# Attention values and low parts of weights on GpSimd, and another order of the opening, in a linear attention and two-MoE kernel

## The chip, the cores and the metric

The kernel runs on one core of one Trainium2 chip. The metric is the device time of one execution in microseconds, from the median of several runs. Everything is in fp32; the large matmuls work on operands split into a high and a low part (fp32r), three products for each.

## What is computed

A gated linear attention (4 batches, 8 heads, 768 positions, 48 channels), then a mixture of 4 experts, then a second feed-forward layer. Setup and shapes are left out:

```python
    for t in range(S):
        state = alpha[:, :, t, :, None] * state + np.einsum('bhd,bhe->bhde', k[:, :, t], v[:, :, t])
        y[:, :, t] = np.einsum('bhd,bhde->bhe', q[:, :, t], state)
...
    x = attn_out.transpose(0, 2, 1, 3).reshape(3072, 384)
    p = domain_probs / (domain_probs.sum(-1, keepdims=True) + 1e-09)
    for e in range(4):
        out += p[:, e:e + 1] * (np.maximum(x @ w1[e], 0.0) @ w2[e])
...
    h = out @ w_in
    return (h * np.clip(h + 3.0, 0.0, 6.0) / 6.0) @ w_out
```

## The kernel before

The attention is cut into 12 units of 256 positions of one batch (`n` = 0 to 11). The state recurrence of a unit is unrolled as a tree: chunks of 8 positions in each partition are worked out elementwise (`chunk`), and the levels above (4, 8, 16, 32 chunks of positions, `tree`) by small matmuls on TensorE, with masks and scalings between them.

The pieces have short names, and strings of names fix their order. In `chunk`: `p0` to `p3` are products of q and k of the innermost three levels, `r0` to `r2` their sums over channels (a reduction, `dg`), `u0`, `u1`, `kk`, `kq`, `tp` scale q and k by alpha for the next level, `cp` copies on ACT, and `y0` to `y5` multiply the values `v` by those sums and add them into `y8`. In `tree`: `T_tp`, `T_k0`, `T_k1`, `T_q0`, `T_q1` transpose on TensorE and copy out of PSUM (ACT; for `qt` of unit 0 VectorE, line 326), `tls` makes products of the gates, `Sc` copies one level's operands (ACT), `C` are that level's matmuls, `Su` scales `kt` and `qt` (VectorE, line 356), `M` multiplies the mask in, `K` transposes the scaled keys, `U` makes the state updates, `Y` brings `y8` into PSUM, `L` adds the levels, `Z` carries the state on, `ST` adds the state's share, `X` orders the copies behind it, `A` stores the unit's result into `x_d` in DRAM, `R` loads it back as MoE input, and `XS` splits it into high (ACT, line 775) and low part (VectorE, line 776).

The MoE goes in three phases over slices of 256 hidden columns. Phase 0 handles the first seven slices of weights (`S0`) while the attention runs: in each step one `mm1` (9 matmuls into `ph`), the relu on ACT into `hh` (line 808), `hl` on VectorE (line 811), and `mm2` of the step before (9 matmuls into `po`). Between the steps stands one group of attention pieces (`GROUP`, `BETWEEN`) and its `rest` (`CHUNK`), seven groups to a unit. The first two periods of 14 steps have 256 token columns each and the later ones 512; two units belong to a period. In the first period the weights also arrive: `load_w`, then `split_w`, whose high part is copied on ACT (line 756) and whose low part VectorE subtracts (line 757), one of 14 such tiles a step from the second step on. They are loaded into the two buffers of `rawp` and four pieces of room lent by x's tiles (`early`, `again`).

Inside the manual schedule (line 916) VectorE, ACT, TensorE and SP carry out their instructions in program order; GpSimd's few (masks, memsets, later two multiplications of `decode`) are ordered by the scheduler. All DMAs are issued by SP, which waits in order too. The opening (lines 949 to 983) is written out by hand: unit 0 from beginning to end, then the elementwise part of unit 1, with `busy(n)` for n idle matmuls (each of two passes) that keep TensorE going. `raw` tiles of q, k, alpha and v have one buffer each, so that the next unit's load waits for the last reader.

Of the kernel before, what the change touches and what calls it, by code (L numbers as in the profile page):

```python
# [18 lines left out]
P = 128  # L19


class Attention:
# [29 lines left out]
        "-X tls", "Sc0 Su0", "Sc1 Su1", "Sc2 M0 Su2", "Sc3 Su3", "M2", "Z0 Z1 Z2 Z3",  # L52
    )
    CHUNK = (
        "y0 y1 y2 y3 y4 y5", "-A +p0 +r0", "+p1 +p2 +r1", "-R +u0", "+u1 +cp +kk +kq", "+tp +p3 +r2", "-XS",
    )

    def __init__(self, ctx, tc, q, k, v, alpha, y_d, psum_pool, psum_tag, reload, split):
# [97 lines left out]
    def chunk(self, n):  # L156

        nc, D = self.nc, self.D  # L160
        ve = nc.vector
        tt = ve.tensor_tensor
        r = self.rawt[n]
        wtags = ("w", "w", "w") if n else ("asb0", "w", "asb1")
        mul, add = ALU.mult, ALU.add
        y8 = self.y8.rearrange("p i h d -> p h i d")[:, :, :, 0:D]
        st = {}

        def hm(ap, w):
            return ap.rearrange("p h (m w) d -> p (h m) w d", w=w)  # L170

        q, k, a = r["q"], r["k"], r["a"]
        q2, k2, a2 = hm(q, 2), hm(k, 2), hm(a, 2)
        q4, k4 = hm(q, 4), hm(k, 4)

        def wtile(x):
            cols = 1024 if wtags[x].startswith("asb") else 768
            w = self.wk.tile([P, cols], F32, tag=wtags[x], name=f"w{x}_{n}")[:, 0:768]
            st[x] = w
            return w  # L180

        def ptile(x):
            return self.wk.tile([P, 768], F32, tag="pr", name=f"pr{x}_{n}")

        def padded(t, h, part):

            return t.rearrange("p (m w) h d -> p h m w d", w=4)[:, h, :, 2 * part : 2 * part + 2, 0:D]

        def p0():
            tt(wtile(0).rearrange("p (h i d) -> p h i d", h=2, d=D), q, k, op=mul)  # L190

        def p1():
            tt(q, q, a, op=mul)

        def p2():

            tt(wtile(1)[:, 0 : 8 * D].rearrange("p (x d) -> p x d", d=D), q2[:, :, 1, :], k2[:, :, 0, :], op=mul)

        def u0():
            tt(q2[:, :, 1, :], q2[:, :, 1, :], a2[:, :, 0, :], op=mul)  # L200

        def u1():
            tt(k2[:, :, 0, :], k2[:, :, 0, :], a2[:, :, 1, :], op=mul)
            st["t1"] = self.wk.tile([P, 8, D], F32, tag="t1", name=f"t1_{n}")
            tt(st["t1"], a2[:, :, 0, :], a2[:, :, 1, :], op=mul)

        def cp():
            for h in range(2):
                nc.scalar.copy(padded(self.kp, h, 1), k4[:, 2 * h : 2 * h + 2, 2:4, :])
                nc.scalar.copy(padded(self.qp, h, 0), q4[:, 2 * h : 2 * h + 2, 0:2, :])  # L210

        def side(z, zp, y):
            t1v = st["t1"].rearrange("p (x w) d -> p x w d", w=2)
            for h in range(2):
                hs = slice(2 * h, 2 * h + 2)
                tt(
                    padded(zp, h, 1 - y),
                    z[:, hs, 2 * (1 - y) : 2 * (1 - y) + 2, :],
                    t1v[:, hs, y, :].unsqueeze(2).to_broadcast([P, 2, 2, D]),
                    op=mul,  # L220
                )

        def kk():
            side(k4, self.kp, 1)

        def kq():
            side(q4, self.qp, 0)

        def tp():
            tpv = self.tp.rearrange("p x h d -> p h x d")[:, :, :, 0:D]  # L230
            t1h = st["t1"].rearrange("p (h x w) d -> p h x w d", h=2, w=2)
            tt(tpv, t1h[:, :, :, 0, :], t1h[:, :, :, 1, :], op=mul)

        def p3():

            wv = wtile(2).rearrange("p (x t s d) -> p x t s d", x=4, t=2, s=2)
            for i in range(2):
                tt(
                    wv[:, :, i],
                    q4[:, :, 2 + i, :].unsqueeze(2).to_broadcast([P, 4, 2, D]),  # L240
                    k4[:, :, 0:2, :],
                    op=mul,
                )

        def reduced(x, n_):
            dg = self.wk.tile([P, 16], F32, tag=f"dg{x}", bufs=2, name=f"dg{x}_{n}")
            ve.tensor_reduce(
                dg[:, 0:n_], st[x][:, 0 : n_ * D].rearrange("p (x d) -> p x d", d=D), op=add, axis=AX.X
            )
            st[f"dg{x}"] = dg  # L250

        def y0():
            tt(y8, r["v"], st["dg0"].rearrange("p (h i) -> p h i", h=2).unsqueeze(3).to_broadcast([P, 2, 8, D]), op=mul)

        def y1():
            pv = ptile(0)[:, 0 : 8 * D].rearrange("p (x d) -> p x d", d=D)
            tt(pv, hm(r["v"], 2)[:, :, 0, :], st["dg1"][:, 0:8].unsqueeze(2).to_broadcast([P, 8, D]), op=mul)
            yv = y8.rearrange("p h (m w) d -> p h m w d", w=2)[:, :, :, 1, :]
            tt(yv, yv, pv.rearrange("p (h m) d -> p h m d", h=2), op=add)

        def y2():
            st["pv"] = ptile(1).rearrange("p (x t s d) -> p x t s d", x=4, t=2, s=2)
            y3_(0)

        def y3_(i):
            dv = st["dg2"].rearrange("p (x t s) -> p x t s", t=2, s=2)
            tt(st["pv"][:, :, i], hm(r["v"], 4)[:, :, 0:2, :], dv[:, :, i, :].unsqueeze(3).to_broadcast([P, 4, 2, D]), op=mul)

        def y3():
            y3_(1)  # L270

        def y4():
            pv = st["pv"]
            tt(pv[:, :, :, 0, :], pv[:, :, :, 0, :], pv[:, :, :, 1, :], op=add)

        def y5():
            yv = y8.rearrange("p h (m w) d -> p h m w d", w=4)
            pw = st["pv"].rearrange("p (h m) t s d -> p h m t s d", h=2)
            for i in range(2):
                tt(yv[:, :, :, 2 + i, :], yv[:, :, :, 2 + i, :], pw[:, :, :, i, 0, :], op=add)  # L280

        return dict(
            p0=p0, p1=p1, p2=p2, p3=p3, r0=lambda: reduced(0, 16), r1=lambda: reduced(1, 8),
            r2=lambda: reduced(2, 16), u0=u0, u1=u1, cp=cp, kk=kk, kq=kq, tp=tp,
            y0=y0, y1=y1, y2=y2, y3=y3, y4=y4, y5=y5,
        )

# [3 lines left out]
    def tree(self, n):  # L291
# [196 lines left out]
        def A():  # L488
            for j in range(2):
                ys = wk(f"ys{j}", [P, NP, P])  # L490
                nc.scalar.copy(ys, s["py"][j])
                for h in range(2):
                    nc.sync.dma_start(
                        self.y_d.rearrange("(r h e) t -> h e r t", r=NP, h=2)[h][:, :, n * U + P * j : n * U + P * j + P],
                        ys[64 * h : 64 * h + D],
                    )
# [32 lines left out]
    def rest(self, g):  # L529
        n, k = divmod(g, self.H)  # L530
        self.run(n, self.CHUNK[k])

        if k == 1:
            self.load(n + 1, "v")
            self.load_vt(n)
        if k == 5:
            self.load(n + 2, "qka")
            self.load_vd(n + 1)
# [3 lines left out]
def tile_gla__then__moe__then__moe2(  # L542
# [206 lines left out]
    def split_w(y, i, eng):  # L749
        raw = raws.pop((y, i))  # L750
        pool = wpb if S0 <= i < S0 + SB or S1 <= i < S1 + SB else wpa
        hi, lo = (pool.tile([P, 3 * SL], F32R, tag=f"w{y}{z}", name=f"w{y}{z}_{i}") for z in "hl")
        if eng is nc.gpsimd:
            eng.tensor_copy(hi, raw)
        else:
            nc.scalar.copy(hi, raw)
        eng.tensor_tensor(lo, raw, hi.bitcast(F32), op=sub)
        wts[(y, i)] = [t.rearrange("p (j f) -> p j f", j=KT if y == 0 else 2) for t in (hi, lo)]

# [153 lines left out]
            nc.sync.dma_start(out[r0 : r0 + P, :], o)  # L913


    ctx.enter_context(tc.manual_schedule(engines={mybir.EngineType.DVE, mybir.EngineType.Activation, mybir.EngineType.PE, mybir.EngineType.SP}))
    at_ctx = ExitStack()
    at = Attention(at_ctx, tc, q, k, v, alpha, x_d, psa, "psa", lambda n: load_x(0, n), lambda n: split_x(0, n))
    NU = at.NU
# [16 lines left out]
    def u(names, n=0):  # L936
        at.run(n, names)

    def sw(y, i):
        split_w(y, i, nc.vector)  # L940

    idle = ps1.tile([P, 512], F32, tag="ps1", name="idle")

# [3 lines left out]
            pe.matmul(idle[:, 0:P], at.ident, at.ident, start=True, stop=True)  # L947

    busy(30)
    u("p0 p1 p2 u0 u1 cp kk kq tp T_tp T_k0 T_k1")  # L950
    u("T_q0 tls T_q1")
    busy(6)
    u("p3 r0")
    at.load(1, "qka")
    load_w(0, 1)
    load_w(1, 1)
    load_w(0, 2)
    load_w(1, 2)
    u("Sc0 C0 Su0 Sc1 r1")
    busy(5)  # L960
    u("y0 C1 Su1 Sc2 y1")
    busy(5)
    u("M0 Su2 Sc3 r2 C2 Su3")
    busy(5)
    u("C3 y2 M2 K0 K1 y3 y4 y5 U Y L0 L1 L2 L3 X Z0 Z1 Z2 Z3 ST")
    sw(0, 0)
    busy(20)
    sw(1, 0)
    u("p0 r0", 1)
    u("A R")  # L970
    at.load(1, "v")
    at.load_vd(1)
    u("p1 p2 r1 u0 u1 cp kq kk tp p3 r2", 1)
    emit_probs()
    load_p(0)
    load_p(1)
    load_w(0, 3)
    sw(0, 1)
    again(0)
    load_w(1, 3)  # L980
    at.load(2, "qka")
    u("T_tp T_k0 T_k1 tls", 1)
    u("XS")


    g = at.H + 1
# [149 lines left out]
```

## Time and profile before

| | |
|---|---|
| median of 3 runs | 1408.17 us |
| lowest, highest | 1406.34, 1408.73 us |
| the profiled execution | 1408.03 us, span 1406.2 us |
| busy: PE, VectorE, ACT, GpSimd | 1376.1, 835.1, 460.8, 83.3 us |
| first MoE matmul of a step | 50.49 us from the span's start |

Times are microseconds from the start of the span. PE is TensorE's matmul queue, DVE is VectorE, ACT ScalarE, POOL GpSimd, SPq SyncE's queue of DMA issues. The page has the busy time of each engine and 40 slices of 35 us; the trace can be asked for windows, for groups of instructions by line, for waits and for the order of time. `x8` is a count of instructions; in brackets stands the idle time before an instruction and what ended it.

### The profile page before, as it was taken

The page shows a single profiled execution, that of the slowest core. Times are in us where ns is not written, and L with a number is a line of the kernel's source. Part 1 is how long each engine was busy: PE and PEld are TensorE (multiplying, and loading weights), DVE is VectorE, ACT ScalarE, POOL GpSimd, SP SyncE. Part 2 cuts the span into 40 slices and gives each one's busy share as a digit, 9 for nine tenths or more (in the row PEclk, how much of TensorE's full clock was granted, in tenths as well). Part 3 has the DMA queues.
Part 4 walks back from the last instruction along what each step waited for, and adds up shares of the span by engine and source line. Part 5 has one row for each costly group of instructions (what it writes and reads, how often), then busy time and mean ns, then how long its engine had stood idle before and what let it go on. Part 6 is the DMA issues. An engine that isn't in the chain of part 4 may idle for free.

```text
span 1406.2 us, 26187 instructions
## 1 busy us (share of the span) xinstructions
PE 1376.1 (98%) x10914; PEld 1181.5 (84%) x10914; DVE 835.1 (59%) x1511; ACT 460.8 (33%) x841; POOL 83.3 (6%) x125
## 2 busy tenths in 40 slices
PE   7789999999999999999999999999999999999998
PEld 7788888888888888888888888888899999999998
DVE  8899977768776258657576666545533333333332
ACT  3554544443444133211111111113333333333333
POOL 2000000000000001211211121100000000000000
PEclk8799999999999999999999999999999999999999
DMA  6554554335442256514242423223201010101000
GB/s 193 168 151 128 158 139 122 104 111 143 141 113 80 73 168 222 161 53 149 64 140 64 136 78 105 84 84 121 80 1 45 1 45 0 46 1 45 1 23 23
DMA packets 127749, 132.33 MB, mean 94 GB/s; under 512 B 33680, under 2 KB 109456, under 8 KB 127632
## 3 DMA queue, kind: packets, MB, share of 16 engines
q1 hardware_dynamic: 127632, 130.68, 31.1%
q8 instruction: 85, 1.39, 0.4%
q14 instruction: 32, 0.26, 0.1%
HBM read 100.71 MB, written 34.65 MB: 96 GB/s over the span
## 4 chain that ended last, share of the span: by engine, by line
PE 89%; DVE 7%; issue 1%; DMA 1%; ACT 1%; SPq 0%; POOL 0%; DVEq 0%; ACTq 0%; POOLq 0%
PE ph L800 40%; PE po L858 26%; PE po L860 14%; PE py L458 2%; PE py L479 1%; PE pa L368 1%; PE pu L404 1%; PE pk L392 1%; PE pkt L321 1%; DVE qt L356 1%; DVE kt L356 1%; DVE asb L380 1%; PE idle L947 1%; DVE hl L811 1%; PE pqt L321 1%
## 5 line engine op out<-in xcount | busy, mean ns | idle before, releaser
L808 ACT ACTIVATE hh<-ph 128x512 fp32r<-128x512 f32 (+1 forms) x206 | 117.4, 570 | 521.3 <-PE ph L800 514.1
L811 DVE SCALAR_TENSOR_TENSOR hl<-ph,hh 128x512 fp32r<-128x512 f32 (+1 forms) x206 | 134.5, 653 | 245.5 <-ACT hh L808 245.5
L800 PE MATMUL ph<-xh,w0h 128*128 128x512 f32 (+1 forms) x906 | 256.9, 392 | 2.3 <-ACT xh L775 2.0
L800 PE MATMUL ph<-xh,w0l 128*128 128x512 f32 (+1 forms) x906 | 248.2, 383 | 0.0
L800 PE MATMUL ph<-xl,w0h 128*128 128x512 f32 (+1 forms) x906 | 247.8, 382 | 0.0
L858 PE MATMUL po<-hl,w1h 128*128 128x512 f32 (+1 forms) x618 | 232.9, 377 | 6.7 <-DVE hl L811 6.7
L858 PE MATMUL po<-hh,w1h 128*128 128x512 f32 (+1 forms) x618 | 232.8, 377 | 4.5 <-DVE t L901 4.5
L858 PE MATMUL po<-hh,w1l 128*128 128x512 f32 (+1 forms) x618 | 232.5, 376 | 0.0
L800 PEld LDWEIGHTS ph<-xh,w0l 128*128 128x128 f32 x906 | 167.6, 190 | 34.3
L800 PEld LDWEIGHTS ph<-xl,w0h 128*128 128x128 f32 x906 | 167.6, 190 | 33.8
L800 PEld LDWEIGHTS ph<-xh,w0h 128*128 128x128 f32 x906 | 162.0, 190 | 27.5 <-ACT xh L775 2.4
L823 DVE SCALAR_TENSOR_TENSOR g<-g,ph 128x512 f32<-128x512 f32 (+1 forms) x97 | 66.2, 683 | 188.6 <-ACT g L819 188.6
L858 PEld LDWEIGHTS po<-hl,w1h 128*128 128x128 f32 x618 | 117.3, 190 | 28.7 <-DVE hl L811 7.8
L858 PEld LDWEIGHTS po<-hh,w1h 128*128 128x128 f32 x618 | 117.2, 190 | 25.8 <-ACT hh L808 2.9
L858 PEld LDWEIGHTS po<-hh,w1l 128*128 128x128 f32 x618 | 117.4, 190 | 20.9
L860 PE MATMUL po<-w1h,hl 128*128 128x384 f32 x384 | 129.8, 338 | 0.1
L860 PE MATMUL po<-w1h,hh 128*128 128x384 f32 x384 | 129.5, 337 | 0.0
L860 PE MATMUL po<-w1l,hh 128*128 128x384 f32 x384 | 129.0, 336 | 0.0
L819 ACT ACTIVATE g<-ph,three 128x512 f32<-128x512 f32 (+1 forms) x97 | 66.4, 685 | 185.8 <-PE ph L800 183.4
L826 DVE SCALAR_TENSOR_TENSOR hl<-g,hh 128x512 fp32r<-128x512 f32 (+1 forms) x97 | 66.6, 688 | 66.5 <-ACT hh L824 66.5
L824 ACT ACTIVATE hh<-g 128x512 fp32r<-128x512 f32 (+1 forms) x97 | 60.9, 629 | 74.5 <-DVE g L823 74.5
L860 PEld LDWEIGHTS po<-w1h,hh 128*128 128x128 f32 x384 | 72.2, 188 | 4.7 <-ACT hh L824 0.4
(105 smaller groups left out, 1419.3 us busy)
## 6 DMA issues: line engine op xcount, KB each, us to landing
rx<-x_d SPq DMA_DIRECT2D x36, 384.0 KB
vl<-vd SPq DMA_DIRECT2D x96, 96.0 KB
rw<-in_moe_w_dram SPq DMA_DIRECT2D x21, 384.0 KB
pb<-p_d SPq DMA_DIRECT2D x28, 256.0 KB
raw<-in_moe_w_in_dram SPq DMA_DIRECT2D x24, 256.0 KB
raw<-in_moe_w_out_dram SPq DMA_DIRECT2D x24, 256.0 KB
acc_d<-t SPq DMA_DIRECT2D x20, 256.0 KB
rq<-in_q_dram SPq DMA_DIRECT2D x24, 192.0 KB
```

Of the source, the lines that this page charges most:

```text
L321: pe.transpose(pt[:, P * i : P * i + P], src[:, 4 * half + i].rearrange("p h d -> p (h d)"), self.ident)
L356: tt(zv, zv, tlv[:, :, 1 - x].unsqueeze(2).to_broadcast([P, nb, w]), op=mul)
L458: pe.matmul(s["py"][j][64 * h : 64 * h + 64, r, :].rearrange("p (b x w) -> p b x w", x=2, w=w)[:, :, 1, :], self.vl[64 * j : 64 * j + 64, ...
L800: pe.matmul(ph[:, 0:n], w[:, j, fs], x[:, j, cs], start=(o == 0 and j == 0), stop=(o == 2 and j == KT - 1),)
L808: nc.scalar.activation(hh[:, 0:n], ph[:, 0:n], AF.Relu)
L811: nc.vector.scalar_tensor_tensor(hl[:, 0:n], ph[:, 0:n], 0.0, hh[:, 0:n].bitcast(F32), op0=ALU.max, op1=sub)
L819: nc.scalar.activation(g[:, c], ph[:, c], AF.Relu, bias=three)
L823: nc.vector.scalar_tensor_tensor(g[:, c], g[:, c], 6.0, ph[:, c], op0=ALU.min, op1=mul)
L824: nc.scalar.activation(hh[:, c], g[:, c], AF.Copy, scale=1.0 / 6.0)
L826: nc.vector.scalar_tensor_tensor(hl[:, c], g[:, c], 1.0 / 6.0, hh[:, c].bitcast(F32), op0=mul, op1=sub)
L858: pe.matmul(accs[vi][m][:, 0:n], w[:, z, ms], h[:, 0:n], **fl)
L860: pe.matmul(accs[vi][m][:, 0:DM], h[:, ms], w[:, z, :], **fl)
```

## The change

The innermost levels' values (`y0` to `y5`) move from VectorE to GpSimd for all 12 units, and so does `p3` of unit 0. The low parts of phase 0's weights (`sw`) are subtracted on GpSimd; their high parts stay on ACT. Those of the later phases (`get_w`) stay on VectorE. GpSimd joins the manual schedule, so that it too goes in program order. `y2` to `y5` are spread over two more groups, and the load of the next `v` goes two groups later. Half of unit 0's four stores are issued by ACT. The opening's order is another on all engines. In the diff, `y1` to `y5` are left out: in each, every `tt` becomes `gt`, as in `y0`.

```diff
     CHUNK = (
-        "y0 y1 y2 y3 y4 y5", "-A +p0 +r0", "+p1 +p2 +r1", "-R +u0", "+u1 +cp +kk +kq", "+tp +p3 +r2", "-XS",
+        "y0 y1", "-A +p0 +r0 y2 y3", "+p1 +p2 +r1 y4 y5", "-R +u0", "+u1 +cp +kk +kq", "+tp +p3 +r2", "-XS",
     )
...
+        gt = nc.gpsimd.tensor_tensor
...
             for i in range(2):
-                tt(
+                (gt if n == 0 else tt)(
                     wv[:, :, i],
...
         def y0():
-            tt(y8, r["v"], st["dg0"].rearrange("p (h i) -> p h i", h=2).unsqueeze(3).to_broadcast([P, 2, 8, D]), op=mul)
+            gt(y8, r["v"], st["dg0"].rearrange("p (h i) -> p h i", h=2).unsqueeze(3).to_broadcast([P, 2, 8, D]), op=mul)
...
                 for h in range(2):
-                    nc.sync.dma_start(
+                    (nc.scalar if n == 0 and h else nc.sync).dma_start(
...
         if k == 1:
+            self.load_vt(n)
+        if k == 3:
             self.load(n + 1, "v")
-            self.load_vt(n)
...
-        if eng is nc.gpsimd:
-            eng.tensor_copy(hi, raw)
-        else:
-            nc.scalar.copy(hi, raw)
+        nc.scalar.copy(hi, raw)
         eng.tensor_tensor(lo, raw, hi.bitcast(F32), op=sub)
...
-    ctx.enter_context(tc.manual_schedule(engines={mybir.EngineType.DVE, mybir.EngineType.Activation, mybir.EngineType.PE, mybir.EngineType.SP}))
+    ctx.enter_context(tc.manual_schedule(engines={mybir.EngineType.DVE, mybir.EngineType.Activation, mybir.EngineType.PE, mybir.EngineType.SP, mybir.EngineType.Pool}))
...
     def sw(y, i):
-        split_w(y, i, nc.vector)
+        split_w(y, i, nc.gpsimd)
...
     busy(30)
-    u("p0 p1 p2 u0 u1 cp kk kq tp T_tp T_k0 T_k1")
-    u("T_q0 tls T_q1")
-    busy(6)
-    u("p3 r0")
+    u("p0 r0 p1 p2 u0 u1 cp kk T_k0 T_k1 kq tp T_tp p3")
+    u("T_q0 T_q1 tls")
+    busy(10)
+    u("y0")
     at.load(1, "qka")
...
-    u("Sc0 C0 Su0 Sc1 r1")
+    u("Sc0 C0 Su0 Sc1 r1 y1")
     busy(5)
-    u("y0 C1 Su1 Sc2 y1")
+    u("C1 Su1 Sc2 r2 y2")
     busy(5)
-    u("M0 Su2 Sc3 r2 C2 Su3")
+    u("M0 Su2 Sc3 C2 Su3 y3")
     busy(5)
-    u("C3 y2 M2 K0 K1 y3 y4 y5 U Y L0 L1 L2 L3 X Z0 Z1 Z2 Z3 ST")
+    u("C3 M2 K0 K1 y4 y5")
+    busy(4)
     sw(0, 0)
+    sw(1, 0)
+    u("U Y L0 L1 L2 L3 Z0 Z1 Z2 Z3 X ST")
     busy(20)
-    sw(1, 0)
-    u("p0 r0", 1)
+    u("p0 r0 p1", 1)
     u("A R")
+    sw(0, 1)
     at.load(1, "v")
     at.load_vd(1)
-    u("p1 p2 r1 u0 u1 cp kq kk tp p3 r2", 1)
+    u("p2 r1 u0 u1 cp kq kk tp p3 r2", 1)
+    load_w(0, 3)
+    again(0)
+    load_w(1, 3)
+    at.load(2, "qka")
+    u("T_tp T_k0", 1)
+    u("XS")
+    u("T_k1 tls", 1)
     emit_probs()
     load_p(0)
     load_p(1)
-    load_w(0, 3)
-    sw(0, 1)
-    again(0)
-    load_w(1, 3)
-    at.load(2, "qka")
-    u("T_tp T_k0 T_k1 tls", 1)
-    u("XS")
```

## Rows read from the trace of the kernel before

**Rows 1.** The page: its first part, and TensorE's granted clock in 40 slices.
```profile
PE 1376.1 (98%) x10914; PEld 1181.5 (84%) x10914; DVE 835.1 (59%) x1511; ACT 460.8 (33%) x841; POOL 83.3 (6%) x125
...
PEclk8799999999999999999999999999999999999999
```
**Rows 2.** Windows: stretch, its length, busy time of each engine, granted clock, DMA share, GB/s.
```profile
18.00:38.40 20.40, 17.73 (x423) 16.01 (x424) 17.02 (x33) 6.48 (x14) 0.00 (x0) 0.75 0.47 151
...
50.50:121.00 70.50, 61.71 (x1033) 57.17 (x1034) 64.25 (x127) 35.84 (x76) 0.00 (x0) 0.86 0.58 170
121.00:186.40 65.40, 60.92 (x1133) 56.22 (x1133) 59.16 (x126) 32.51 (x77) 0.00 (x0) 0.97 0.55 146
186.40:490.00 303.60, 303.29 (x3930) 246.91 (x3927) 205.47 (x385) 119.50 (x247) 0.00 (x0) 1.00 0.40 112
```
**Rows 3.** Windows again, two short stretches inside the first period.
```profile
57.00:66.70 9.70, 7.53 (x137) 6.58 (x136) 9.15 (x16) 5.09 (x10) 0.00 (x0) 1.00 0.79 264
66.70:76.70 10.00, 8.72 (x77) 8.01 (x67) 9.97 (x20) 4.79 (x11) 0.00 (x0) 0.50 0.45 133
```
**Rows 4.** Waits of TensorE from 50.5 to 121 us: total, times, longest.
```profile
PE po L858 <- DVE hl L811: 5.5, 4, 2.1
```
**Rows 5.** Order of time in the opening, to the state products: start, length, instruction.
```profile
17.18 1.02 DVE L238 TENSOR_TENSOR w<-rq,rk 128x384 f32<-128x384 f32 x2
...
18.05 0.69 PE L368 MATMUL pa<-qc,kc 48*64 48x64 f32 x32 [1.93 <-ACT qc L346]
18.12 0.94 DVE L247 TENSOR_REDUCE dg<-w 128x16 f32<-128x768 f32 x1
...
18.98 0.68 DVE L356 TENSOR_TENSOR kt<-kt,tl 128x512 f32<-128x512 f32 x1
...
36.75 1.61 PE L479 MATMUL py<-qt,sc 48*64 48x64 f32 x48 [0.30 <-issue]
```
**Rows 6.** The same view, from the store of unit 0 to its split.
```profile
38.69 2.20 SPq L493 DMA_DIRECT2D x_d<-ys  x4
...
42.79 0.38 SPq L766 DMA_DIRECT2D rx<-x_d  x1
...
45.73 0.35 DVE L232 TENSOR_TENSOR tp<-t 128x192 f32<-128x192 f32 x1
...
47.72 2.08 ACT L328 COPY kt<-pkt 128x256 f32<-128x256 f32 x4 [0.24 <-PE pkt L321]
...
49.58 0.86 ACT L775 CAST xh<-rx 128x768 fp32r<-128x768 f32 x1
```
**Rows 7.** GpSimd's groups by line: count, busy us, mean ns, idle before.
```profile
L669 POOL TENSOR_TENSOR sq<-hc 128x256 f32<-128x256 f32 x48 | 34.5, 718 | 636.2 <-DVE hc L668 636.2
```
**Rows 8.** Order of time where GpSimd and VectorE meet, beside `decode`.
```profile
532.54 0.72 POOL L669 TENSOR_TENSOR sq<-hc 128x256 f32<-128x256 f32 x1 [1.95 <-DVE hc L668]
532.83 0.72 DVE L674 SCALAR_TENSOR_TENSOR a<-hc,a 128x256 int32<-128x256 int32 x1
...
536.67 0.41 DVE L681 SCALAR_TENSOR_TENSOR a<-sq,a 128x256 f32<-128x256 f32 x1
...
594.50 0.95 DVE L776 TENSOR_TENSOR xl<-rx,xh 128x768 fp32r<-128x768 f32 x1
594.66 1.39 POOL L684 TENSOR_TENSOR a<-a,hc 128x256 f32<-128x256 f32 x1 [4.28 <-DVE hc L683]
```
**Rows 9.** VectorE's groups by line; the last two of a unit's values are from the opening.
```profile
L356 DVE TENSOR_TENSOR kt<-kt,tl 128x512 f32<-128x512 f32 x8 | 5.5, 684 | 0.0
L757 DVE TENSOR_TENSOR w1l<-early_l,w1h 128x768 fp32r<-128x768 f32 x3 | 2.9, 954 | 2.3 <-ACT w1h L756 2.3
L232 DVE TENSOR_TENSOR tp<-t 128x192 f32<-128x192 f32 x2 | 0.7, 349 | 0.0
...
L253 DVE TENSOR_TENSOR y<-rv,dg 128x768 f32<-128x768 f32 x1 | 0.9, 947 | 0.0
L280 DVE TENSOR_TENSOR y<-y,pr 128x192 f32<-128x192 f32 x2 | 0.6, 355 | 0.0
```

More of the change, by code (lines that the diff above doesn't have):

```diff
@@ L252, in y0 @@
         def y0():
-            tt(y8, r["v"], st["dg0"].rearrange("p (h i) -> p h i", h=2).unsqueeze(3).to_broadcast([P, 2, 8, D]), op=mul)
+            gt(y8, r["v"], st["dg0"].rearrange("p (h i) -> p h i", h=2).unsqueeze(3).to_broadcast([P, 2, 8, D]), op=mul)
         def y1():
             pv = ptile(0)[:, 0 : 8 * D].rearrange("p (x d) -> p x d", d=D)
-            tt(pv, hm(r["v"], 2)[:, :, 0, :], st["dg1"][:, 0:8].unsqueeze(2).to_broadcast([P, 8, D]), op=mul)
+            gt(pv, hm(r["v"], 2)[:, :, 0, :], st["dg1"][:, 0:8].unsqueeze(2).to_broadcast([P, 8, D]), op=mul)
             yv = y8.rearrange("p h (m w) d -> p h m w d", w=2)[:, :, :, 1, :]
-            tt(yv, yv, pv.rearrange("p (h m) d -> p h m d", h=2), op=add)
+            gt(yv, yv, pv.rearrange("p (h m) d -> p h m d", h=2), op=add)
         def y2():
@@ L266, in y3_ @@
             dv = st["dg2"].rearrange("p (x t s) -> p x t s", t=2, s=2)
-            tt(st["pv"][:, :, i], hm(r["v"], 4)[:, :, 0:2, :], dv[:, :, i, :].unsqueeze(3).to_broadcast([P, 4, 2, D]), op=mul)
+            gt(st["pv"][:, :, i], hm(r["v"], 4)[:, :, 0:2, :], dv[:, :, i, :].unsqueeze(3).to_broadcast([P, 4, 2, D]), op=mul)
         def y3():
@@ L273, in y4 @@
             pv = st["pv"]
-            tt(pv[:, :, :, 0, :], pv[:, :, :, 0, :], pv[:, :, :, 1, :], op=add)
+            gt(pv[:, :, :, 0, :], pv[:, :, :, 0, :], pv[:, :, :, 1, :], op=add)
         def y5():
@@ L279, in y5 @@
             for i in range(2):
-                tt(yv[:, :, :, 2 + i, :], yv[:, :, :, 2 + i, :], pw[:, :, :, i, 0, :], op=add)
+                gt(yv[:, :, :, 2 + i, :], yv[:, :, :, 2 + i, :], pw[:, :, :, i, 0, :], op=add)
         return dict(
```

## The prediction

> **What bounds the kernel now.** I read the slices of the page first, then the windows, then what TensorE waits for, then the order of time in the opening. The page says PE 98% busy, so at first sight nothing is left [rows 1]. The windows say where the rest lies: from 186.4 to 490 us PE is busy 303.29 of 303.60 us at full clock, and it stays so nearly to the end; no edit of VectorE work there can gain anything. Before that there are three stretches that PE doesn't fill [rows 2]. The opening, until the first MoE matmul at about 50 us, works on one attention unit and then waits for its result to come back from memory. The first period (50.5 to 121 us: 14 steps of 256 columns, weights arriving and being split) has PE busy 61.71 of 70.5 us at a mean granted clock of 0.86, beside a VectorE that is busy 64.25. The second (121 to 186.4, no weights left to split) has PE 60.92 of 65.4 and VectorE 59.16. The wait that ends last in the first period is that for `hl`, made by VectorE: 5.5 us in four waits [rows 4]. The clock is hurt as well: in 57 to 66.7 us PE was busy only 7.53 of 9.7 us, and in the next 10 us the granted clock was 0.50, the lower level (1.2 of 2.4 GHz), although PE had work for 8.72 of them [rows 3]. So up to 186 us VectorE sets the pace, and what is won there is kept, because afterwards PE runs without a gap.
>
> **The prices.** VectorE spends 0.95 us on a low part of weights (line 757) and 4.6 us on the values of one unit: eight instructions of six lines, from 0.95 us for `y0` to 0.36 for each half of `y5` [rows 9]. Busy times of neighbours overlap by some 8% (a 0.95 us instruction is followed 0.87 later), which I take off below. GpSimd multiplies 256 columns in 0.72 us [rows 7]. No row has 768 columns there; three times that, 2.16 us, is the upper end, and 1.9 us is what comes out if 0.12 us of the 0.72 are paid once. A unit's values are 3072 columns in all, so 8.2 to 8.9 us on GpSimd against 4.6 on VectorE.
>
> The price that matters more is a different one. VectorE's line 674 reads two SBUF operands of 256 columns and takes 0.72 us while GpSimd multiplies, started 0.29 us before it; line 681, of the same size and also with two SBUF operands, takes 0.41 alone. The other way round, GpSimd's add of line 684 started 0.16 us after VectorE's 0.95 us subtraction of line 776 and took 1.39 us, ending 0.60 after it [rows 8]. So the two exclude each other: GpSimd's 256 columns keep VectorE's two-operand instructions out for about 0.60 us, which makes 1.8 us for 768 columns. That gives 7.2 us per unit, of 12 times 256 columns. Instructions with one operand in PSUM (`hl`, the mask, `finish`) or a single one (reductions) are not of that kind. The Trainium skill's "SBUF — State Buffer", section "Who interferes with whom", has the same as a rule: a Vector instruction with two SBUF inputs contends with a GpSimd instruction that reads SBUF, and whoever starts first blocks the other for the whole instruction. Rows 8 agree; by that rule alone, each displaced low part would cost VectorE up to 1.8 us for 0.95 saved, and the first period would get longer, by the upper bound of its sum below.
>
> **Opening, until the store of the first unit.** `p3` and `r0` stand between 17.18 and 18.98 us on VectorE ahead of the first scaling (`Su0`) [rows 5]. `r0` goes into the wait for alpha, `p3` to GpSimd: 1.8 us. The copies of `qt` now precede `tls`, and `T_k0`, `T_k1` precede `tp`, so that operands are there by then; the first `Sc0` no longer waits for the products of `tls`. `y0` and `y1` leave the chain of scalings (18.98 to 28.3 us): 2.0 us more. Against it stand GpSimd's `p3`, `y0`, `y1`, `y2`, `y3`, seven instructions that lock 7.2 us, each able to stop one scaling; most of `y0` falls beside PSUM copies. Bounds 0 to 7.2; I take 2. The state products, which began at 36.75, come 1.8 us earlier (3.8 earlier to 3.4 later). `y2` to `y5` and `M2` end before their reader on PE as long as GpSimd is less than about 2 us late; the earlier identity and the other counts of idle matmuls cost nothing, since real work ends the wait in each case. The low parts of the first two weights now lock 3.6 us beside `Z0` to `Z3`; 128 small matmuls run there and cover some 1.6 us.
>
> **Store and reload.** SP issues four stores in 2.20 us and the reload at 42.79 [rows 6]. Two now go from ACT's queue, where the second copy of `ys` stands behind the first of them: 0.5 us gained, bounds 0 and 1.1. The reload then issues near 40.5. When it landed before is not shown; it was no later than 49.58, 6.8 us after its issue, so now by 47.3 at the latest.
>
> **First split of x.** ACT splits x at 49.58, behind the copies of `T_tp`, `T_k0` and `T_k1`, which wait for `tp` of unit 1 (45.73) [rows 6]. `T_k1`'s half of the 2.08 us goes behind the split: 1.04 us. `tp` itself comes earlier by the two low parts that left VectorE (1.9) and by the 1.8 of above, and later by what three low parts on GpSimd block (0 to 5.4; I take 1.5): 43.5. From there 3.85 less 1.04 gives 46.3, 3.3 us before 49.58. Bounds: 0.6 later, 6 earlier. SP's queue loses the wait for the probabilities ahead of the loads of unit 2, whose readers are late enough in both orders; ACT gains `T_k1` behind the split, in front of the first `hh`, with 1.5 us of VectorE idle there as cover.
>
> **First period.** VectorE loses eleven low parts and two units' values, 10.5 + 9.3, less 8%: 18.2 us, leaving 46. GpSimd locks 11 x 1.8 + 2 x 7.2 = 34.2 us. VectorE's remaining two-operand instructions are 15 groups, from line 356's 5.5 us (twice) to line 232's 0.7, 30.9 us, some 28.4 start to start [rows 9]. If no lock meets another, PE is the bound: 61.71 x 0.86, 53 us, 17 less than now. If every locked microsecond stops VectorE, 46 + 34 = 80, 10 more. In between: a two-operand instruction comes about every 1.1 us, so a 1.8 us lock nearly always catches one and holds it about 1 us, a 0.9 us lock half as often and for a quarter of a microsecond: 13 x 1 + 14 x 0.25, some 16 us. 46 + 16 = 62 against 64.25: I take 2 us less. The nearest rows are the 0.31 and 0.65 us that rows 8 show for one collision each.
>
> **Second period.** Two units' values less 8% are 8.5 us off VectorE, 14.4 us of locks come; half of them, as above, 7: 1.5 less. PE can't gain more than the 4.5 us that it is idle; I take 1 (bounds 4.5 less, 5.9 more). The later load of `v` has four groups of cover, some 20 us. After 186.4: nothing, since PE is full and VectorE (205 of 304 us) has room for 7.2 us per unit.
>
> **Sum.** -3.3 - 2 - 1 = -6.3 us. The profiled execution took 1408.03 us (span 1406.2); the median of the runs is 1408.17. So 1402.
>
> **Rivals.** (a) Zero-sum: GpSimd takes from VectorE through the lock what it gives, and the opening's gain is eaten by collisions with `p3` and the three low parts. For it: rows 8, and GpSimd needs 8.2 us for 4.6. Against it: the two low parts and `T_k1` leave ACT's and VectorE's queue ahead of the split whatever the lock does. 1407. The skill's "Perfetto Trace Analysis", "Optimizing Scalar/DVE Operations", says just this, that moving work between the two might not help because they share a read port; rows 8 show the sharing, not the result. (b) The lock becomes the bound of the first period, and the kernel gets slower. 34.2 + 28.4 = 62.6 us fit into 70.5; they no longer do when 768 columns lock 2.2 us instead of 1.8 (strided values, a rounded output, which no row has on GpSimd). At 2.5 us the sum is 47.5 + 28.4 = 76, 5.4 more than now; with 1 us of the opening left, 1412. (c) Locks seldom meet, VectorE really drops to some 50 us, the lower clock goes with the waits: 10 in the first period, 3 in the second, 4 at the start: 1391.
>
> **Chances.** My forecast (1396 to 1405) 0.52, (a) 0.18, (b) 0.15, (c) 0.15. About 0.2%, 2.8 us, is what a measurement of this kernel can tell from no change: faster 0.67, same 0.18, slower 0.15. The range, 1388 to 1412, leaves out the far part of (c) and what lies beyond (b).
>
> **What would show it.** The split of x (line 775) near 46 us; `Su0` near 17.2; the first period about 2 us shorter, with line 757 on GpSimd near 2 us, longer where it met VectorE, and lines 356 and 193 on VectorE with means above 0.68 and 0.95. PE full from about 180 us. The sum is wrong if line 757 on GpSimd takes more than 2.5 us alone, if the split of x comes after 49 us, or if PE has gaps after 190 us.

## The result and the profile after

| | before | after |
|---|---|---|
| median | 1408.35 us | 1416.95 us |
| lowest, highest of 4 runs each | 1406.34, 1408.73 | 1415.06, 1420.09 |
| the profiled execution, its span | 1408.03, 1406.2 us | 1416.48, 1414.7 us |
| ratio, 95% interval | | 1.0069 [1.0051, 1.0086] |

The kernel became slower, by 0.69% or 9.7 us as the ratio has it (the two medians differ by 8.6). The forecast was 1402, and the range up to 1412 doesn't hold the time. Ratios here and below are formed from the fast runs; one of ten executions of the opening's order alone, 4680.78 us, is not among them. Line numbers are each kernel's own: lines 356, 775 and 811 of before are 357, 774 and 810 of after. The page of after (busy time, share, count), against [rows 1]:

```profile
PE 1379.4 (98%) x10930; PEld 1183.8 (84%) x10930; DVE 820.5 (58%) x1399; ACT 462.3 (33%) x841; POOL 209.8 (15%) x237
```

VectorE lost 15 us of busy time although it lost some 68 us of work (12 units of 4.6 us and 14 low parts of 0.95): its other instructions became longer. The windows are those of [rows 2], moved to about the same steps: stretch, length, busy time of PE, PE's weight loads, VectorE, ACT and GpSimd, granted clock, DMA share, GB/s.

```profile
50.60:126.00 75.40, 61.38 (x970) 56.19 (x974) 61.00 (x101) 35.71 (x77) 43.16 (x31) 0.84 0.51 150
126.00:193.40 67.40, 61.69 (x1173) 56.84 (x1173) 57.02 (x106) 33.77 (x79) 19.29 (x20) 0.97 0.56 149
193.40:500.00 306.60, 305.91 (x3959) 248.97 (x3959) 198.14 (x337) 120.26 (x248) 46.87 (x48) 1.00 0.40 111
```

The first stretch grew, and VectorE is idle in 14.4 us of it, against 6.2 before. Afterwards PE is full, as before. Step by step (the start of the n-th `hl` on VectorE, read from the order of time of both kernels) the loss is +1.2 us at step 0, -0.1 at 5, +1.9 at 6, +3.9 at 7, +6.5 at 9, +7.0 at 13 and still +7.0 at 28, +8.1 at 30; the spans differ by 8.5. So up to the first `hl` 1.2 us were lost where 3.3 were to be won, which steps 1 to 5 made up for; 6.6 us were lost between steps 5 and 9, where one unit ends and the next begins, and nothing from step 13 to 28. (The second window has 2.0 us of the loss only because it begins before step 14, which came 4.5 us late.) Such leads and lags of single profiles are good to some 2 to 3 us: the kernels below that share one opening without GpSimd split x anywhere from 43.59 to 46.21 us.

What happened between steps 5 and 9 can be read from after's order of time, from TensorE's waits and from one window, first of after and then of before:

```profile
78.12 1.46 DVE L233 TENSOR_TENSOR tp<-t 128x192 f32<-128x192 f32 x1
79.51 2.65 DVE L239 TENSOR_TENSOR w<-rq,rk 128x384 f32<-128x384 f32 x2
```
```profile
PE ptt L310 <- DVE sc L434: 3.5, 1, 3.5
```
```profile
85.00:100.00 15.00, 13.51 (x218) 12.40 (x219) 4.30 (x13) 8.12 (x19) 5.43 (x5) 0.79 0.51 134
```
```profile
85.00:100.00 15.00, 11.73 (x205) 10.89 (x198) 12.33 (x25) 9.81 (x22) 0.00 (x0) 1.00 0.57 140
```

Two low parts on GpSimd (77.54 to 81.28 us) stretched `tp` and `w` from 0.35 and 1.02 us [rows 5, 9], 2.7 us in sum. `Z`, which stands behind them, came late, and TensorE waited 3.5 us for its `sc`, a wait that before does not have. After the wait the granted clock fell: 0.79 in the mean of these 15 us, against 1.00 before, some 3 us by my estimate (15 times 0.21).

The opening of after in order of time (start, length, engine, line, tiles, count, idle before), to be read beside [rows 5, 6]:

```profile
10.74 2.31 POOL L239 TENSOR_TENSOR w<-rq,rk 128x384 f32<-128x384 f32 x2 [0.35 <-DVE rk L204]
11.16 2.10 DVE L217 TENSOR_TENSOR kp<-rk,t 128x192 f32<-128x192 f32 x2
13.02 1.58 POOL L254 TENSOR_TENSOR y<-rv,dg 128x768 f32<-128x768 f32 x1
13.19 1.90 DVE L217 TENSOR_TENSOR qp<-rq,t 128x192 f32<-128x192 f32 x2
...
19.80 0.68 DVE L357 TENSOR_TENSOR kt<-kt,tl 128x512 f32<-128x512 f32 x1
...
22.54 1.38 POOL L260 TENSOR_TENSOR y<-y,pr 128x384 f32<-128x384 f32 x1
22.97 1.50 DVE L357 TENSOR_TENSOR qt<-qt,tl 128x512 f32<-128x512 f32 x1
...
49.69 0.86 ACT L774 CAST xh<-rx 128x768 fp32r<-128x768 f32 x1
```

Beside `p3` and `y0` on GpSimd, `kp` and `qp` took 2.10 and 1.90 us; with GpSimd idle (in the experiment on the opening's order, below) each takes 0.62:

```profile
11.68 0.62 DVE L217 TENSOR_TENSOR kp<-rk,t 128x192 f32<-128x192 f32 x2
```

`Su0` of after starts at 19.80 instead of the forecast 17.2, and the split of x at 49.69, where it stood before (49.58).

One meeting in the first period (same columns):

```profile
57.66 1.85 POOL L756 TENSOR_TENSOR w1l<-early_h,w1h 128x768 fp32r<-128x768 f32 x1 [5.05 <-ACT w1h L755]
57.90 0.42 DVE L810 SCALAR_TENSOR_TENSOR hl<-ph,hh 128x256 fp32r<-128x256 f32 x1 [0.22 <-ACT hh L807]
58.24 2.09 DVE L191 TENSOR_TENSOR w<-rq,rk 128x768 f32<-128x768 f32 x1
```

`hl`, with one operand in PSUM, passes untouched. The product of q and k, two SBUF operands, starts behind `hl` and ends 0.82 us after the low part: 2.09 us for what takes 0.95 alone. VectorE's groups in 50.6 to 126 us say the same in means (busy us, mean ns, idle before):

```profile
L357 DVE TENSOR_TENSOR kt<-kt,tl 128x512 f32<-128x512 f32 x8 | 7.2, 897 | 6.7 <-ACT kc L347 6.7
L810 DVE SCALAR_TENSOR_TENSOR hl<-ph,hh 128x256 fp32r<-128x256 f32 x14 | 5.8, 417 | 5.4 <-ACT hh L807 5.4
L381 DVE TENSOR_TENSOR asb<-pa,mask 128x512 f32<-128x512 f32 x8 | 5.1, 682 | 0.0
...
L204 DVE TENSOR_TENSOR rk<-rk,ra 128x384 f32<-128x384 f32 x2 | 3.7, 1841 | 0.0
```

`kt` went from 684 to 897 ns [rows 9]; lines 810 and 381, each with a PSUM operand, did not move.

### The profile page after: what moved, and what is told of

It is laid out like the page before. It is cut to its first block, busy times and chain, and to the rows that moved or that the text cites. A ratio compares the mean times of both kernels' runs of the same rounds, so it can differ in the third digit from the quotient of the medians.

```text
span 1414.7 us, 26276 instructions
## 1 busy us (share of the span) xinstructions
PE 1379.4 (98%) x10930; PEld 1183.8 (84%) x10930; DVE 820.5 (58%) x1399; ACT 462.3 (33%) x841; POOL 209.8 (15%) x237
## 4 chain that ended last, share of the span: by engine, by line
PE 86%; DVE 11%; ACT 1%; issue 1%; DMA 0%; SPq 0%; DVEq 0%
PE ph L799 40%; PE po L857 25%; PE po L859 14%; PE py L480 1%; PE py L459 1%; DVE qt L357 1%; DVE kt L357 1%; DVE dg L248 1%; PE pa L369 1%; DVE asb L381 1%; PE pkt L322 1%; DVE hl L810 1%; PE pqt L322 1%; DVE w L191 1%; PE pk L393 1%
```

## The experiments

The theory: GpSimd's instructions that read SBUF shut out VectorE's with two SBUF operands; these stand on the chain, while the work that VectorE gave away was done where it would have waited anyway. Rivals: the new order on VectorE costs the time, and GpSimd none; or GpSimd's results are simply late, and something waits for them. Each ratio is to the kernel before on the same chip; 0.001 is 1.4 us. Runs of different ratios are subtracted below; that part of the difference which the intervals leave open is 2 to 3 us. The expectations are in us of the median, which stands beside each ratio; the kernel before took 1405.76 to 1406.31 us beside them.

One rival can be read from the traces. In after's list of waits, this is the only one of TensorE, ACT or VectorE that GpSimd ended (TensorE's weight loads share it), and so it is in the other kernels with values or low parts on GpSimd:

```profile
PE idle L946 <- POOL ident masks.py:199: 1.4, 1, 1.4
```

It stands at the start of the span, before any of the moved work. So none of these engines waited for a result that GpSimd brought late.

**All values, `p3` and the low parts back on VectorE, in the new order**

```diff
-        gt = nc.gpsimd.tensor_tensor
+        gt = nc.vector.tensor_tensor
-        split_w(y, i, nc.gpsimd)
+        split_w(y, i, nc.vector)
```

> The changed kernel with its values, its p3 and its low parts back on VectorE: only the order of the opening, the spread of y0 to y5 over three groups, the two stores on ACT's queue and GpSimd in program order are left of the change. Lock theory (GpSimd's reads shut out VectorE's instructions with two SBUF operands, and that alone is what the change loses): the opening is no longer stretched, the split of x comes 1 to 3 us before 49.6, the first period is as long as before, total 1403 to 1407. Order theory (the new order itself costs: stores on ACT, T_k1 behind the split, the probabilities late): total 1412 or more, with the 12th to 14th hl late in the same way as in the changed kernel.

Measured 1.0080 [1.0065, 1.0095], 1417.73 us. This spoke for the rival: slower with GpSimd idle. But the step starts say where: `hl` is 5.9 us earlier than before at step 0, 6.0 at 7, 3.9 at 13, then 0.4 later at 28. The opening gains; something in the loop costs, and neither theory had that.

**Only the low parts back; only the values and `p3` back**

Both on the changed kernel.

```diff
-        split_w(y, i, nc.gpsimd)
+        split_w(y, i, nc.vector)
```

> The changed kernel with only the low parts of the weights back on VectorE; values and p3 stay on GpSimd. Lock theory: GpSimd's 14 instructions of two units in the first period lock 14.4 instead of 34 us, so VectorE's two-operand instructions are stretched by 3 to 5 us there instead of some 14; its released time (about 8 us) lies at the unit's border where VectorE has little else to do. Total 1407 to 1412. Order theory: 1412 or more, as with the order alone. If the values are the whole loss: 1416.

Measured 1.0045 [1.0029, 1.0060], 1412.07 us.

```diff
-        gt = nc.gpsimd.tensor_tensor
+        gt = nc.vector.tensor_tensor
```

> The changed kernel with values and p3 back on VectorE; the 14 low parts stay on GpSimd. Lock theory: each 1.8 us low part stops one two-operand instruction for about 1 us, the most harmful part of the change, since it comes in the middle of the steps: total 1410 to 1415. Late-GpSimd theory (the loss comes from low parts that queue behind the values on GpSimd and reach TensorE late): nothing is queued in front of them any more, total 1403 to 1407.

Measured 1.0128 [1.0113, 1.0143], 1424.70 us, above both theories. The two parts don't add up: against the kernel with neither on GpSimd (1.0080), the values there win and the low parts there lose. With the finding of that run this asked for a separation of the order's own parts.

**The low parts alone, on the kernel before**

```diff
-        split_w(y, i, nc.vector)
+        split_w(y, i, nc.gpsimd)
```

> The kernel before with nothing changed but the engine of the 14 low parts (GpSimd, in program order). Lock theory: VectorE's two-operand instructions grow by about 10 us in sum in the first period, VectorE loses 10.5 us of its own, so 1407 to 1413. Order theory: the loss belongs to the order and not to GpSimd, so 1404 to 1408.

Measured 1.0042 [1.0027, 1.0057], 1411.87 us. Without any new order the low parts on GpSimd cost 5.9 us.

**The opening's order alone; the spread alone**

The first has the new opening, with everything on VectorE and the old loop; the second is the kernel before with the new `CHUNK` and the later load of `v`, as the change has them. The diff is of the first, against after; `gt` and `sw` are as in the first experiment.

```diff
     CHUNK = (
-        "y0 y1", "-A +p0 +r0 y2 y3", "+p1 +p2 +r1 y4 y5", ...
+        "y0 y1 y2 y3 y4 y5", "-A +p0 +r0", "+p1 +p2 +r1", ...
...
         if k == 1:
+            self.load(n + 1, "v")
             self.load_vt(n)
-        if k == 3:
-            self.load(n + 1, "v")
```

> The order of the opening alone (with the two stores on ACT's queue and GpSimd in program order); y0 to y5 stand in one group as before and everything is on VectorE. Theory of three parts (the opening's order gains about 6 us as long as GpSimd doesn't collide in it; spreading the values costs about 9 us when VectorE has them; the low parts on GpSimd cost 5): the split of x at 43.6 us as with the order and spread together, and 6 us less kept to the end, total 1400 to 1402. Rival (what is won in the opening is lost again because VectorE sets the pace up to 180 us): total 1405 to 1408, with the lead of the first hl gone by the 25th.

Measured 0.9982 [0.9972, 0.9991], 1403.63 us: faster than before, by less than expected. ACT's part of its order of time:

```profile
45.26 1.12 ACT L329 COPY kt<-pkt 128x256 f32<-128x256 f32 x2 [0.24 <-PE pkt L322]
46.16 0.86 ACT L773 CAST xh<-rx 128x768 fp32r<-128x768 f32 x1
```

The split stands behind two copies instead of four, 3.4 us earlier than in [rows 6], and `hl` is 3.9 to 4.0 us earlier from step 6 to step 30: what the opening wins is kept, in the profiled execution; timed, 2.5 us are.

> The kernel before with nothing changed but the places of y2 to y5 (one and two groups later, behind p0, r0 and p1, p2, r1) and of the load of v; all on VectorE. Theory of three parts: the spread puts 1.1 us of values ahead of hl in two more groups of each unit; where a step is short of VectorE, TensorE waits for hl to free ph, in the later periods too: 1412 to 1418. Rival (the opening's order is at fault): 1405 to 1408.

Measured 1.0130 [1.0115, 1.0145], 1424.40 us, +18.3 us and above the expectation. The piece of the change that I had costed at nothing. Windows from the third period on, first of the spread alone, then of the opening's order alone (columns as above):

```profile
193.00:500.00 307.00, 300.40 (x3934) 243.63 (x3933) 205.46 (x388) 119.44 (x247) 0.00 (x0) 1.00 0.38 108
```
```profile
182.00:490.00 308.00, 307.74 (x3963) 250.61 (x3958) 206.56 (x387) 120.12 (x248) 0.00 (x0) 1.00 0.39 111
```

VectorE's busy time is about the same, yet PE loses 6.6 us in the one and 0.3 in the other. TensorE's waits in the spread kernel from 195 us on (total, times, longest), and the stretch of VectorE behind them:

```profile
PE ph L801 <- DVE hl L812: 4.8, 9, 1.2
```
```profile
205.29 0.68 DVE L812 SCALAR_TENSOR_TENSOR hl<-ph,hh 128x512 fp32r<-128x512 f32 x1
205.89 0.94 DVE L193 TENSOR_TENSOR rq<-rq,ra 128x768 f32<-128x768 f32 x1
...
207.93 0.55 DVE L274 TENSOR_TENSOR pr<-pr 128x384 f32<-128x384 f32 x1
208.51 0.63 DVE L280 TENSOR_TENSOR y<-y,pr 128x192 f32<-128x192 f32 x2
209.06 1.28 DVE L380 TENSOR_TENSOR asb<-pa,mask 128x512 f32<-128x512 f32 x2
...
211.46 0.68 DVE L812 SCALAR_TENSOR_TENSOR hl<-ph,hh 128x512 fp32r<-128x512 f32 x1
```

This group now has `y4` and `y5` (lines 274 and 280) in front of its `hl`, the one before it `y2` and `y3`. The two `hl` are 6.2 us apart with VectorE never idle between them. In the opening's order alone the same group's `hl` are these:

```profile
192.38 0.69 DVE L809 SCALAR_TENSOR_TENSOR hl<-ph,hh 128x512 fp32r<-128x512 f32 x1 [0.51 <-ACT hh L806]
...
197.43 0.68 DVE L809 SCALAR_TENSOR_TENSOR hl<-ph,hh 128x512 fp32r<-128x512 f32 x1
```

They are 5.05 us apart, VectorE is not idle between them there either, and the group before has 0.51 us left. So the group was full already, and what came in made it longer. Whether the later load of `v` has a share in this wasn't tried.

**Values of units 1 to 11 on GpSimd, then eleven low parts as well**

Both on the changed kernel; unit 0's values, `p3` and the first three low parts are on VectorE, so that GpSimd has nothing in the opening.

```diff
-        gt = nc.gpsimd.tensor_tensor
+        gt = nc.gpsimd.tensor_tensor if n else tt
```

> The changed kernel with all low parts and unit 0's p3 and values on VectorE: only the values of units 1 to 11 are on GpSimd. Theory of three parts: the opening has no collision, 6 us gained there; values on GpSimd cost 2 to 4 us by collisions in the first two periods and free the later ones: total 1401 to 1405. Lock theory in its full form (values on GpSimd always give back what they free): 1406 or more.

Measured 1.0009 [1.0000, 1.0019], 1407.25 us, where the lock theory in its full form had it.

```diff
-        split_w(y, i, nc.gpsimd)
+        split_w(y, i, nc.vector if (y, i) in ((0, 0), (1, 0), (0, 1)) else nc.gpsimd)
```

> The changed kernel with GpSimd out of the opening: unit 0's p3 and values and the first three low parts are on VectorE; the other eleven low parts and the values of units 1 to 11 stay on GpSimd. Theory of three parts: the opening's 6 us come back, the first period's loss of 6 us stays: 1407 to 1411, 5 to 7 us below the changed kernel. If the collisions in the opening don't matter (first hl as late as with them): 1414 or more.

Measured 1.0049 [1.0034, 1.0064], 1412.59 us, just above the expectation. With the opening's order at 0.9982 this makes a chain to the whole change: -2.5 us for the order, +3.8 for values with their spread, +5.6 for eleven low parts, and +2.8 for GpSimd in the opening, from 1.0049 to 1.0069, whose intervals overlap.

**The values left out; the values on GpSimd without the spread**

On the opening's order alone. The first leaves out `y0` to `y5` of units 1 to 11, so it measures what it is worth to free VectorE of them, with no GpSimd at all.

```diff
-            y0=y0, y1=y1, y2=y2, y3=y3, y4=y4, y5=y5,
+            **({} if n else dict(y0=y0, y1=y1, y2=y2, y3=y3, y4=y4, y5=y5)),
```

> The order of the opening alone, as run before, with the values of units 1 to 11 left out (no engine computes them; y8 keeps those of unit 0). It measures what VectorE's 4.6 us per unit are worth at most, with no collision. Border theory (the values stand at the border of two units, where VectorE waits for TensorE's transposes and ACT's copies anyhow): 1402 to 1404, at most 1.5 us below the opening alone. Sum theory (VectorE's busy time sets the pace up to 180 us, as the prediction had it): 4 to 8 us below it, 1396 to 1400.

Measured 0.9968 [0.9958, 0.9978], 1401.94 us, against 0.9982 with them: 2.0 us for 50 us of VectorE's work (eleven units of 4.6), and the intervals meet. VectorE's two largest idle times in 47 to 182 us of this kernel, then the counterparts in the one with the values:

```profile
L809 DVE SCALAR_TENSOR_TENSOR hl<-ph,hh 128x256 fp32r<-128x256 f32 (+1 forms) x29 | 12.3, 425 | 6.8 <-ACT hh L806 6.8
L357 DVE TENSOR_TENSOR kt<-kt,tl 128x512 f32<-128x512 f32 x16 | 10.9, 684 | 15.7 <-ACT kc L347 15.7
```
```profile
L809 DVE SCALAR_TENSOR_TENSOR hl<-ph,hh 128x256 fp32r<-128x256 f32 x28 | 11.7, 418 | 1.9 <-ACT hh L806 1.9
...
L357 DVE TENSOR_TENSOR kt<-kt,tl 128x512 f32<-128x512 f32 x16 | 11.0, 685 | 2.6 <-ACT kc L347 2.6
```

Where the values were, VectorE now waits for ACT's `kc` and `hh`: 13.1 and 4.9 us more, of some 21 us that the values took in this stretch.

```diff
-        gt = nc.vector.tensor_tensor
+        gt = nc.gpsimd.tensor_tensor if n else tt
```

> The order of the opening alone, with the values of units 1 to 11 on GpSimd, in one group as before (not spread). Lock theory: the collisions of the values cost the 3 to 4 us that they cost when spread, 1405 to 1408. If the spread was what cost there too: 1402 to 1404.

Measured 1.0014 [1.0005, 1.0024], 1408.02 us. GpSimd's values cost 6.5 us more than no values at all. Spread over three groups (1.0009) or not (1.0014) makes no difference that these runs can tell, so the spread costs only where VectorE does the work. Lines 337 (`tls`) and 428 (the products `sd` of `Z`) in the same stretch, with the values on GpSimd (first) and on VectorE (second):

```profile
L337 DVE TENSOR_TENSOR tl<-tl 128x128 f32<-128x128 f32 (+3 forms) x20 | 13.3, 663 | 0.5
...
L428 DVE TENSOR_TENSOR sd<-sc,tl 128x192 f32<-128x192 f32 x14 | 9.1, 651 | 0.4
```
```profile
L428 DVE TENSOR_TENSOR sd<-sc,tl 128x192 f32<-128x192 f32 x14 | 5.0, 356 | 0.4
...
L337 DVE TENSOR_TENSOR tl<-tl 128x128 f32<-128x128 f32 (+3 forms) x20 | 4.4, 219 | 0.5
```

These two lines alone are 13.0 us longer beside GpSimd's values; half of that, 6.5 us, is what the kernel paid for all eleven units.

**Eleven low parts: subtracted, written without reading, in four pieces**

All on the opening's order alone, which has them on VectorE (0.9982).

```diff
-        split_w(y, i, nc.vector)
+        split_w(y, i, nc.vector if (y, i) in ((0, 0), (1, 0), (0, 1)) else nc.gpsimd)
```

> The order of the opening alone, with the eleven later low parts on GpSimd, values on VectorE in one group. Lock theory: 4 to 6 us above the opening alone, 1407 to 1411, with VectorE's lines 191, 204 and 357 stretched by GpSimd's low parts. If the low parts were harmful only beside values on GpSimd: 1402 to 1404.

Measured 1.0011 [1.0002, 1.0021], 1407.61 us.

In the next two GpSimd writes zeros three times in place of each subtraction, so that it writes as long but reads nothing; the low parts are left out. In the first nothing holds the writes back, and they ran at 10 to 35 us, in the opening; in the second ACT's one column (the line with `nc.scalar.copy`, which the first doesn't have) holds each until its weights are there.

```diff
-        eng.tensor_tensor(lo, raw, hi.bitcast(F32), op=sub)
+        if eng is nc.gpsimd:
+            nc.scalar.copy(lo[:, 0:1], hi[:, 0:1].bitcast(F32))
+            for _ in range(3):
+                eng.memset(lo.bitcast(F32), 0.0)
+        else:
+            eng.tensor_tensor(lo, raw, hi.bitcast(F32), op=sub)
```

> The order of the opening alone, with the subtraction of the eleven later low parts left out: GpSimd sets them to zero instead, three times each (about 2 us of GpSimd, writing only, reading nothing). Lock theory: GpSimd that only writes doesn't stop VectorE's two-operand instructions; these keep 0.68 and 0.95 us, and VectorE has 10 us less to do: 1396 to 1403. If it is GpSimd's length or its order that delays the weights: as with the real low parts on GpSimd, 1407 to 1411.

Measured 0.9931 [0.9914, 0.9947], 1396.05 us.

> The order of the opening alone, with the subtraction of the eleven later low parts left out; GpSimd writes zeros instead, three times (2.3 us), and must wait for ACT, which first writes one column of the same tile: same place, same time and a little more length than the real low part, but nothing is read. Lock theory: as with the writes ahead of time, 1394 to 1400, VectorE's line 357 at 0.68 us. Place and length theory (any 2 us on GpSimd between ACT's copy and TensorE's use costs): 1405 to 1410.

Measured 0.9927 [0.9911, 0.9943], 1396.28 us. The same place and a longer time on GpSimd, and the kernel is 11.8 us faster than with the subtractions. Order of time of the second, where a write and a scaling overlap, and its group of line 204; then that of the subtractions:

```profile
52.56 2.33 POOL L758 MEMSET w1l<- 128x768 f32 x3 [42.34 <-ACT w1l L756]
52.70 0.69 DVE L357 TENSOR_TENSOR kt<-kt,tl 128x512 f32<-128x512 f32 x1
...
L204 DVE TENSOR_TENSOR rk<-rk,ra 128x384 f32<-128x384 f32 x2 | 1.1, 549 | 0.0
```
```profile
L204 DVE TENSOR_TENSOR rk<-rk,ra 128x384 f32<-128x384 f32 x2 | 3.7, 1840 | 0.0
```

549 ns beside writes, 1840 beside reads; both instructions of line 204 overlap with GpSimd in either trace. Against the opening's order alone, nine of VectorE's two-operand instructions at 46 to 117 us are longer beside the subtractions, by 12.0 us in sum, and none is beside the writes. This is the run that settles the theory for the low parts: it is the reading, not GpSimd's being late or busy. For the values no such run was made; there the stretched lines above speak for the same cause. The Trainium skill's "SBUF — State Buffer", section "Who interferes with whom", states it so: VectorE's second SBUF operand conflicts with a GpSimd instruction that reads SBUF, not with one that only writes. Both halves agree with these two runs; the price, 1.07 us of kernel time for each of eleven low parts, is these runs' own.

```diff
-        eng.tensor_tensor(lo, raw, hi.bitcast(F32), op=sub)
+        for c in range(0, 3 * SL, 192) if eng is nc.gpsimd else (0,):
+            cs_ = slice(c, c + 192) if eng is nc.gpsimd else slice(0, 3 * SL)
+            eng.tensor_tensor(lo[:, cs_], raw[:, cs_], hi[:, cs_].bitcast(F32), op=sub)
```

> The order of the opening alone, with the eleven later low parts on GpSimd in four instructions of 192 columns each instead of one of 768. Lock theory with arbitration between instructions: a VectorE instruction waits for one piece of some 0.5 us, not for 2 us, and so gets in earlier, but may meet several pieces: 1402 to 1407. If GpSimd's whole reading time is lost in any case: 1408 to 1411, as in one piece or worse by the added instructions.

Measured 0.9977 [0.9966, 0.9988], 1403.64 us, 4.8 us faster than whole. Groups of GpSimd and VectorE:

```profile
L757 POOL TENSOR_TENSOR w1l<-early_h,w1h 128x192 fp32r<-128x192 f32 x12 | 8.8, 766 | 44.6 <-ACT w1h L754 44.6
```
```profile
L357 DVE TENSOR_TENSOR kt<-kt,tl 128x512 f32<-128x512 f32 x8 | 7.3, 914 | 0.0
...
L204 DVE TENSOR_TENSOR rk<-rk,ra 128x384 f32<-128x384 f32 x2 | 1.2, 612 | 0.0
```

GpSimd works longer (8.8 us for three low parts, 5.5 in one piece each), yet line 204 is back at 612 ns: VectorE gets in between two pieces. Not every line gains, `kt` has 914 ns where whole low parts leave 812: more instructions are met, 22 in place of nine, but none is longer by more than 0.44 us, and the sum falls from 12.0 to 8.2 us. This kernel and the opening's order alone both beat before and after; the runs can't tell the two from each other.

## Why the prediction was wrong

**What was right.** The opening's order: the split of x was forecast for 46.3 us and came at 46.16 once GpSimd was out of the way; the forecast 3.3 us were 4.0 in the profile, 2.5 timed. That it came within 0.2 us is luck: with the same opening the ten runs without GpSimd in it have the split from 43.59 to 46.21, and with the old order the spread alone has it at 47.28, not 49.58. PE has no gaps after 190 us. The exclusion read from [rows 8], which instructions it touches, and its price for low parts: eleven times about 1 us was forecast, 12.0 us of stretch and 11.8 us of time measured. Taking the eleven low parts off VectorE was forecast at 9.7 us and was worth 7.7 (0.9927 against 0.9982).

**The step that failed: the value of what VectorE gave away.** "VectorE loses eleven low parts and two units' values", less 8%, was put against the locks one for one. For the values that was wrong. Left out altogether they are worth 2.0 us where the two periods' forecast had 17. They stood at the border of two units, where VectorE waits for `kc` from ACT as soon as they are gone. The locks of the values had about the forecast's size, some 12 us there and 13.0 in lines 337 and 428 alone (in the run without the spread), but 6.5 us of them reached the time. 2.0 against 6.5 is a loss where 17 against 12 was a gain. VectorE's busy time of the first period came out as forecast, 62 and 61.0 us; only the period took 75.4. I had taken that sum for its pace, and that premise, that VectorE sets the pace up to 186 us, failed: in the rest of the period VectorE waited, 14.4 us. So the place decides: the low parts' 12.0 us of stretch cost 11.8 us, the values' 13.0 cost 6.5, and work taken away at a wait returned 2.0 of 17.

Added up from runs: low parts -7.7 + 11.8, values -2.0 + 6.5, that is +8.6 us, against -3 in the forecast for both periods. The opening adds 0.3 (-2.5 + 2.8) where -3.3 were forecast. That makes 8.9 of the measured 9.7, within what the intervals leave open.

**Second step: GpSimd in the opening.** `p3` and the values were taken at 2 us of bounds 0 to 7.2, the low parts there at 1.5. By the trace the first made `kp` and `qp` 2.8 us longer and the scalings some 3, and the low parts made `Z`'s `sd` 1.3 longer and unit 1's scaling of line 201 1.1: 8.1 us in sum where 3.5 were taken. The prediction had `y0` mostly beside the PSUM copies, and nothing beside `kp` and `qp`. Timed, taking GpSimd out of the opening gives back 2.8 us (1.0069 against 1.0049), as much as the order wins, but the two intervals overlap; the split of x says it more clearly, at 49.69 and 49.99 us in the two kernels with `p3` and `y0` to `y5` of unit 0 on GpSimd, and at 46.21 or earlier in those with the same order and GpSimd out of the opening.

**Third: the spread at nothing.** It is nothing while GpSimd has the values, as in the change, so it doesn't explain the loss; with VectorE it costs 18.3 us. The prediction left out what already stands in the groups that receive `y2` to `y5`.

**The rivals.** (b) had the side, slower, and the mechanism. Its condition, 2.2 us or more for 768 columns, did not hold: where it met nothing, a low part took 1.81 to 1.85 us on GpSimd, and locks and two-operand work still fit into the period by their sums. (a) had the opening right, that its gain is eaten. (c), that locks seldom meet, is excluded: in after's first period 18 of VectorE's instructions were longer, by 14.3 us in sum, near the forecast 16. Of the signs named in the prediction one showed, the split of x after 49 us. That results come too late from GpSimd is excluded by the traces, in which nothing waits for them, and for the low parts by the run with writes as well. Part of the price passes through TensorE's granted clock (0.84 in after's first period, 0.93 in that of the opening's order alone). Between steps 5 and 9 that part is some 3 us; for the rest it is open.

## What to carry to other kernels

Price work that is moved off an engine by what stands behind it: if the engine waits there for another one, the move is worth next to nothing, however long the instruction (here 2.0 of 50 us), and the way to know before moving is to leave it out. Put no GpSimd instruction that reads SBUF beside a chain of VectorE work with two SBUF operands; if it must be there, cut it into pieces that let VectorE in. Work laid into another group of the same engine has to be checked against what that group must deliver on time.

## What the runs showed of the hardware

GpSimd took 1.81 to 1.85 us for a dense subtraction of two operands of 768 columns where it met nothing, but 1.47 for 768 columns with one operand broadcast (line 254) and 0.74 for writing them with a constant. Three such writes in a row, 2.33 us, did not lengthen a VectorE instruction beside them (0.69 us). Four pieces of 192 columns kept GpSimd busy 60% longer than one of 768 (8.8 against 5.5 us) and cost the kernel 4.8 us less.
